# Attention and a Fourier-gated layer on one core: head pairs in seven key tiles, a written order on TensorE, folded transforms, a staged first batch

## The chip, the cores and the metric

The kernel runs on one NeuronCore of a Trainium2 chip. The core has TensorE (PE in the profile; its weight loads are PEld), VectorE (DVE), ScalarE (ACT), GpSimd (POOL) and SyncE (SP, which only issues DMAs here). Each engine takes its own instructions in the order in which they stand in its queue, and waits on semaphores for the others. The metric is the device time of one execution in microseconds.

## The reference

Batch 8, 12 heads, 448 positions, head size 64, so a model width D of 768. All inputs and the output are float32; the kernel's products run in bfloat16.

```python
scores = scale * np.matmul(q, k.transpose(0, 1, 3, 2))
m = np.max(scores, axis=-1, keepdims=True)
e = np.exp(scores - m)
attn = e / (np.sum(e, axis=-1, keepdims=True) + np.exp(-m) + 1e-09)
return np.matmul(attn, v)
...
x = attn_out.transpose(0, 2, 1, 3).reshape(B, S, H * D)
...
proj = x @ w_proj                      # three parts of 768 columns: x1, x2, x3
X2 = np.fft.rfft(x2, n=S, axis=1)
H = np.fft.rfft(filter_fft, n=S, axis=0)[None, :, :]
x2_conv = np.fft.irfft(X2 * H, n=S, axis=1)
y = x1 * x2_conv * x3
return (y @ w_out)
```

Both kernels leave out the maximum, since exp(s) / (sum of exp(s) + 1) is the same number. The Fourier transforms are matrix products with tables of cosines and sines.

## The kernel before

Setup builds the tables in four pages (cosine and sine, frequencies 0 to 127 and 128 to 224), loads filter, w_out and w_proj in float32 over SP and casts them on DVE, and computes the filter's spectrum `hh`.

Per batch, `attn_load` brings q, k and v through POOL's queue, cast to bfloat16 by the DMA: 12 loads of 112 positions × 12 heads × 64, in runs of 256 bytes. Positions are cut into four tiles of 112. For each of the six head pairs, `attn_pair_scores` transposes q and k of both heads on PE into one 128-row tile, copies k into two tiles that are zero in the other head's half (`kTA`, `kTB`, cleared by POOL), and makes 8 score products of 448 columns, each with one exp on ACT (`ET`). `attn_pair_O` makes 32 products of 65 columns (64 of v and a column of ones for the row sum) into `oph`, and DVE divides (`rec`, `xb`). `attn_finish` transposes the result into `xT`.

`hyena_chunks` is the dense part of a batch, in six pieces: `proj_x1`, `proj_x3`, `proj_x2` (x2 with positions on the rows), `spectrum` (32 products `xr`, `xi`, and for each pair of pages six DVE products with `hh`), `idft_gate` (24 products `cps` of 448 columns) and `write_out` (48 products `ops`). `run_attention_with_chunks` places one piece of batch b behind the scores of each pair of batch b + 1. The order of instructions on every engine is then made by the tile framework's scheduler from that program. PSUM is one pool with two banks for each of four uses: transposes (`tr`), scores (`sc`), attention output (`op`), dense (`hy`).

Of the kernel before, what the change touches and what calls it, by code (L numbers as in the profile page):

```python
# [10 lines left out]
AF = mybir.ActivationFunctionType  # L12
# [10 lines left out]
NDT = D // 128  # L23
SCALE = 1.0 / float(np.sqrt(DH))
DCH = 384

PAGE_K0 = [0, 0, 128, 128]
PAGE_W = [128, 128, 97, 97]
PAGE_COS = [True, False, True, False]
FT_COL0 = [0, 128, 256, 353]  # L30
FT_NCOL = 450
# [3 lines left out]
def kernel(  # L35
# [12 lines left out]
    TWO_PI = float(2.0 * np.pi)  # L48
    SIN_SHRINK = 1.0 - 2e-6
    sin_scale = (TWO_PI / S) * SIN_SHRINK  # L50
    sin_bias = -float(np.pi) * SIN_SHRINK
# [7 lines left out]
    ident_f32 = const.tile([128, 128], F32, name="ident_f32")  # L59
    make_identity(nc, ident_f32)  # L60
    sin_bias_t = const.tile([128, 1], F32, name="sin_bias_t")
    exp_bias = const.tile([128, 1], F32, name="exp_bias")
    nc.vector.memset(sin_bias_t, sin_bias)
    nrow = const.tile([128, S], F32, name="nrow")
    kvec = []

    ft = wts.tile([SP, NST, FT_NCOL], BF16, name="ft")
    bt = wts.tile([128, 4, S], BF16, name="bt")
    wproj_bf = wts.tile([128, NDT, 3 * D], BF16, name="wproj_bf")
    wout_bf = wts.tile([128, NDT, D], BF16, name="wout_bf")  # L70
    filt_bf = wts.tile([SP, NST, D], BF16, name="filt_bf")
    hh = wts.tile([128, 4, D], BF16, name="hh")

    ld = ctx.enter_context(tc.tile_pool(name="ld", bufs=4))
    vextp = ctx.enter_context(tc.tile_pool(name="vextp", bufs=2))
    qktp = ctx.enter_context(tc.tile_pool(name="qktp", bufs=2))
    etp = ctx.enter_context(tc.tile_pool(name="etp", bufs=12))
    xbp = ctx.enter_context(tc.tile_pool(name="xbp", bufs=2))
    xtp = ctx.enter_context(tc.tile_pool(name="xtp", bufs=2))
    hyp = ctx.enter_context(tc.tile_pool(name="hyp", bufs=1))  # L80
    ytp = ctx.enter_context(tc.tile_pool(name="ytp", bufs=1))
    otp = ctx.enter_context(tc.tile_pool(name="otp", bufs=2))
    small = ctx.enter_context(tc.tile_pool(name="small", bufs=3))
    stmp_w = ctx.enter_context(tc.tile_pool(name="stmp_w", bufs=2))

    def setup_constants_and_weights():
        with tc.tile_pool(name="stmp", bufs=1) as stmp:
# [426 lines left out]
```

## Time and profile before

| | us |
|---|---|
| median of 3 runs (621.81, 623.59, 626.63) | 623.59 |
| span of the profiled execution | 615.7 |
| PE matmul busy | 541.6 (88%), 4336 instructions |
| DVE busy | 347.8 (56%) |
| ACT busy | 278.1 (45%) |
| POOL busy | 145.6 (24%) |
| HBM read, written | 43.84 MB, 11.01 MB |

The profile is of one execution; its span runs from its first to its last instruction, and its own time with what lies around the span is not among the runs' times, whose median is 7.9 us above the span. A row of a group reads: line, engine, operation, output<-inputs with their shapes, xcount, then busy us and mean ns of one, then idle time of the engine before it and what ended it. "L291" is line 291 of the kernel. The mean of a matmul is its latency: matmuls overlap, and the chain's pieces (a length for several matmuls in a row) show their pace. Rows of stages give busy us and count for each engine, the granted PE clock, the mean DMA share and GB/s.

### The profile page before, as it was taken

Reading aid. Unit: us, or ns where it says so; the run is one execution under the profiler, and the core shown is the slowest. Engines: PE = TensorE matmul, PEld = TensorE weight load, DVE = VectorE, ACT = ScalarE, POOL = GpSimd, SP = SyncE. Lnnn points to the kernel's source line nnn. Section 1 sums busy time; section 2 is a strip of 40 time slices with the busy share of each in tenths; the row PEclk is TensorE's granted clock in tenths of the full one; section 3 lists DMA queues with packets and bytes.
Section 4 is the critical chain, followed back from the end, with each engine's and each line's share of the span. In section 5 each row is a group of like instructions: output and inputs, shape, how many; then the busy total and the mean of one; then the engine's idle time right before and its main releaser. Section 6 shows DMA issues by size and latency. Waiting matters only on the chain.

```text
span 615.7 us, 10809 instructions
## 1 busy us (share of the span) xinstructions
PE 541.6 (88%) x4336; PEld 367.8 (60%) x4336; DVE 347.8 (56%) x929; ACT 278.1 (45%) x527; POOL 145.6 (24%) x237
## 2 busy tenths in 40 slices
PE   0127889999999899989999899989999999989977
PEld 0014665766667575757667566757576666757544
DVE  4743545475464935394656746393647546493572
ACT  0106775436436255536355453545453643735112
POOL 3533263033211522033301531052212300100000
PEclk9997898999999999999999999999999999999999
DMA  9999097029900985069900991088901920002002
GB/s 235 235 209 204 1 92 46 1 16 98 113 1 2 79 124 25 2 40 97 91 1 1 91 124 12 1 55 117 56 1 13 101 69 1 1 1 90 2 1 89
DMA packets 137810, 39.04 MB, mean 63 GB/s; under 512 B 131424, under 2 KB 131424, under 8 KB 137760
## 3 DMA queue, kind: packets, MB, share of 16 engines
q0 software_dynamic: 130560, 16.52, 46.6%
q1 hardware_dynamic: 7200, 21.83, 12.0%
q8 instruction: 34, 0.56, 0.4%
q14 instruction: 16, 0.13, 0.1%
HBM read 43.84 MB, written 11.01 MB: 89 GB/s over the span
## 4 chain that ended last, share of the span: by engine, by line
PE 78%; DVE 11%; DMA 6%; ACT 4%; issue 1%; DVEq 0%
PE scps L271 14%; PE oph L291 12%; PE ops L444 10%; PE pps L360 10%; PE pps L345 9%; PE pps L331 9%; PE cps L424 4%; ACT ET L277 4%; DMA w<-in_moe_w_proj_dram 4%; PE xr L378 3%; PE xi L387 3%; DMA f<-in_moe_filter_fft_dram 3%; DVE t L399 2%; PE ktps L255 1%; DVE t L408 1%; PE xtps L315 1%
## 5 line engine op out<-in xcount | busy, mean ns | idle before, releaser
L277 ACT ACTIVATE ET<-scps,exp_bias 112x448 bf16<-112x448 f32 x384 | 217.3, 635 | 214.9 <-PE scps L271 209.3
L291 PEld LDWEIGHTS <-ET 112*112 112x112 bf16 x1536 | 98.0, 133 | 18.1 <-issue 5.3
L291 PE MATMUL oph<-vext,ET 112*112 112x65 bf16 x1536 | 101.8, 217 | 0.7
L299 DVE TENSOR_SCALAR rec<-oph 112x4 f32<-112x4 f32 x96 | 15.2, 158 | 137.4 <-PE oph L291 136.3
L262 POOL MEMSET kTA<- 64x448 bf16 x48 | 22.5, 469 | 236.8 <-PE scps L271 223.0
L444 PE MATMUL ops<-wout_bf,yT 128*112 128x384 bf16 x384 | 74.3, 326 | 0.0
L271 PE MATMUL scps<-qT,kTB 128*112 128x448 bf16 x192 | 69.0, 359 | 4.9 <-DVE kTB L265 2.7
L360 PE MATMUL pps<-wproj_bf,xT 128*112 128x384 bf16 x384 | 72.9, 326 | 0.0
L271 PE MATMUL scps<-qT,kTA 128*112 128x448 bf16 x192 | 69.4, 361 | 3.4 <-DVE kTA L264 1.6
L331 PE MATMUL pps<-xT,wproj_bf 128*128 128x448 bf16 x288 | 71.8, 354 | 0.1
L345 PE MATMUL pps<-xT,wproj_bf 128*128 128x448 bf16 x288 | 64.6, 352 | 0.0
L444 PEld LDWEIGHTS <-yT 128*112 128x112 bf16 x384 | 48.5, 129 | 15.9 <-issue 1.8
L360 PEld LDWEIGHTS <-xT 128*112 128x112 bf16 x384 | 48.6, 129 | 15.7 <-issue 1.5
L424 PE MATMUL cps<-bt,yhat 128*128 128x448 bf16 x192 | 44.9, 351 | 9.2 <-DVE t L408 9.0
L367 ACT CAST x2n<-pps 112x384 bf16<-112x384 f32 x64 | 29.9, 480 | 37.6 <-PE pps L360 37.6
L451 ACT COPY osb<-ops 112x384 f32<-112x384 f32 x64 | 29.8, 480 | 37.1 <-PE ops L444 26.4
L338 DVE CAST x1T<-pps 128x448 bf16<-128x448 f32 x48 | 29.9, 624 | 28.9 <-PE pps L331 28.6
L352 DVE CAST x3T<-pps 128x448 bf16<-128x448 f32 x48 | 30.0, 624 | 23.4 <-PE pps L345 22.3
L345 PEld LDWEIGHTS <-wproj_bf 128*128 128x128 bf16 x288 | 27.9, 98 | 24.8 <-issue 2.8
L301 DVE TENSOR_TENSOR xb<-oph,rec 112x256 bf16<-112x256 f32 x96 | 40.1, 418 | 1.9
L331 PEld LDWEIGHTS <-wproj_bf 128*128 128x128 bf16 x288 | 27.5, 98 | 20.9 <-issue 3.0
L227 POOL DMA_DIRECT2D vext<-in_v_dram x32 | 31.4, 986 | 32.4 <-PE xtps L315 28.2
(68 smaller groups left out, 632.2 us busy)
## 6 DMA issues: line engine op xcount, KB each, us to landing
out_dram<-osb SPq DMA_DIRECT2D x32, 336.0 KB, 2.7
w<-in_moe_w_proj_dram SPq DMA_DIRECT2D x12, 576.0 KB, 7.0
qf<-in_q_dram POOLq DMA_DIRECT2D x32, 168.0 KB, 5.4
kf<-in_k_dram POOLq DMA_DIRECT2D x32, 168.0 KB, 5.2
vext<-in_v_dram POOLq DMA_DIRECT2D x32, 168.0 KB, 6.1
wo<-in_moe_w_out_dram SPq DMA_DIRECT2D x6, 384.0 KB, 5.7
f<-in_moe_filter_fft_dram SPq DMA_DIRECT2D x4, 336.0 KB, 4.6
```

The source lines that it names most:

```text
L227: nc.gpsimd.dma_start(vext[:, st, :, 0:DH], v[b, :, st * SP : (st + 1) * SP, :].rearrange("h p d -> p h d"),)
L271: nc.tensor.matmul(scps, kT[:, i * SP : (i + 1) * SP], qT[:, :],)
L277: nc.scalar.activation(e, scps, AF.Exp, scale=SCALE, bias=exp_bias[:SP, 0:1])
L291: nc.tensor.matmul(oph[:, j, :], et[u][i][:, j * SP : (j + 1) * SP], vext[:, i, h, :], start=(i == 0), stop=(i == NST - 1),)
L301: nc.vector.tensor_tensor(xb[:, :, h, :], oph[:, :, 0:DH], rec[:].unsqueeze(2).to_broadcast([SP, NST, DH]), op=ALU.mult,)
L331: nc.tensor.matmul(pps, wproj_bf[:, kt, dt * 128 : (dt + 1) * 128], xT[:, kt, :], start=(kt == 0), stop=(kt == NDT - 1),)
L338: nc.vector.tensor_copy(hb["x1T"][:, dt, :], pps)
L345: nc.tensor.matmul(pps, wproj_bf[:, kt, 2 * D + dt * 128 : 2 * D + (dt + 1) * 128], xT[:, kt, :], start=(kt == 0), stop=(kt == NDT - 1),)
L352: nc.vector.tensor_copy(hb["x3T"][:, dt, :], pps)
L360: nc.tensor.matmul(pps[:SP, :DCH], xT[:, kt, st * SP : (st + 1) * SP], wproj_bf[:, kt, D + ch * DCH : D + (ch + 1) * DCH], start=(kt == 0) ...
L424: nc.tensor.matmul(cps, yhat[:W, pg, dt * 128 : (dt + 1) * 128], bt[:W, pg, :], start=(pg == 0), stop=(pg == 3),)
L444: nc.tensor.matmul(ops_[:SP, :DCH], yT[:, dt, st * SP : (st + 1) * SP], wout_bf[:, dt, ch * DCH : (ch + 1) * DCH], start=(dt == 0), stop=( ...
```

## The change

The kernel is written anew around the same mathematics.

- **Attention.** The 896 keys of a head pair are cut into seven tiles of 128: three of each head, and one that holds the last 64 keys of both. `kz` is a ring of three tiles with fixed zero halves. A pair makes 7 score products; two heads' products of a tile go into two neighbouring banks and share one exp of 896 elements. `attn_out` works on 128 queries at a time (the last tile overlaps the one before) with 128-column weights: 7 products for each of 4 query tiles, in two halves that use the one bank of `op`. Exps take no bias tile. POOL's clearing of `kTA` and `kTB` is gone.
- **Transforms.** `back` folds xT about its ends and middle on DVE (`u`, `w`, `xf`), so that even and odd frequencies, cosine and sine, are four separate blocks of 113 or 112. proj2 works on the folded x. The spectrum takes 8 products, each copied by ACT; the inverse takes 24 products of 224 columns, and ACT and DVE unfold them (`cw`, `cv`).
- **Order.** PE's and POOL's orders are as written; the scheduler orders the rest. `attention(b)` gives 48 units, `dense(b)` 36, each with a cost from a table; after each attention unit dense units of the batch before are put in while `owed` (1.9 times the attention cost) lasts. A last few are left for the next batch.
- **PSUM.** Scores: 2 × 2 banks; `op`: 1; everything else: 3 (`hy`).
- **Loads.** Batch 0's q, k and v come in float32 over SP in runs of 256 to 1024 bytes and are cast by DVE (k), ACT (q) and POOL (v). w_proj, filter and w_out come through POOL's queue, cast by the DMA. Later batches' 13 loads (4 of q, 8 of k, 1 of v) are issued at unit 8 of the batch before.

DVE, the head of the program, where the filter is used for the first time. Before, from the first transposed q to the first division (`w` is a float32 piece of w_proj):

```order
L251 COPY qT<-qtps 128x448 [waits PE_49]
L264 COPY kTA<-ktps 64x448 [waits PE_49]
L265 COPY kTB<-ktps 64x448
L204 CAST wproj_bf<-w_865 128x1152 [waits DMAHW4_49]
L204 CAST wproj_bf<-w_868 128x1152 [waits DMAHW5_49]
L264 COPY kTA<-ktps 64x448 [waits DVE_49,PE_49,Pool_49]
L251 COPY qT<-qtps 128x448 [waits PE_49]
L265 COPY kTB<-ktps 64x448 [waits DVE_49,Pool_49]
L299 TENSOR_SCALAR rec<-oph 112x4 [waits PE_49]
```

Now, from pair 2's transposes to the first division of pair 1 (`uw` is the filter's fold, `filt` the loaded filter, `xps` the transposed output of pair 0):

```order
L330 COPY kz_119<-tps 64x4x128 [waits PE_49]
L331 COPY kz_119<-tps 64x512
L334 COPY qT<-tps 128x4x112
L391 COPY xT<-xps 128x448 [waits PE_49]
L288 TENSOR_TENSOR uw<-filt 113x1536 [waits DMASW6_49,DMASW5_49,DMASW7_49,DMASW4_49,DMASW3_49]
L373 TENSOR_SCALAR rec<-op 128x4 [waits PE_49]
L289 TENSOR_TENSOR uw<-filt 113x1536
L374 RECIPROCAL rec<-rec 128x4 [waits DVE_49]
L375 TENSOR_TENSOR xb<-op,rec 128x2x128 [waits DVE_49]
```

Casts of w_proj pieces stood between the pairs; in their place the fold of the filter, with a wait for five loads of POOL's queue, stands ahead of pair 1's division.

PE, the middle of a batch: before, scores of a pair among the products of x1 of the batch before (`pps`):

```order
L331 MATMUL pps_2015<-xT,wproj_bf 128x448
L271 LDWEIGHTS kTA
L271 MATMUL scps<-qT,kTA 112x448
L331 LDWEIGHTS wproj_bf
L331 MATMUL pps_2015<-xT,wproj_bf 128x448
L271 LDWEIGHTS kTB
L271 MATMUL scps<-qT,kTB 112x448
```

Now, the last two scores of a pair, a unit of proj2 (`xf` is the folded x) and the first products of attn_out:

```order
L346 LDWEIGHTS kz_118
L346 MATMUL sc<-qT,kz_118 128x448
...
L440 LDWEIGHTS xf
L440 MATMUL pps_1004<-wproj_bf,xf 113x384
...
L360 LDWEIGHTS er
L360 MATMUL op<-vr_116,er 128x130
L365 LDWEIGHTS e
L365 MATMUL op<-vn_114,e 128x65
```

Single scores that alternated with single dense products now stand as blocks: four scores, six dense products, then fourteen of attn_out.

The core of the diff:

```diff
-    psum = ctx.enter_context(tc.tile_pool(name="psum", bufs=2, space=bass.MemoryType.PSUM))
+    psc = ctx.enter_context(tc.tile_pool(name="psc", bufs=2, space=bass.MemoryType.PSUM))
+    pop = ctx.enter_context(tc.tile_pool(name="pop", bufs=1, space=bass.MemoryType.PSUM))
+    phy = ctx.enter_context(tc.tile_pool(name="phy", bufs=3, space=bass.MemoryType.PSUM))
...
     def attn_load(b):
...
+            )
+        for u in range(2):
+            c = slice(64 * u, 64 * u + 64)
+            for t in range(3):
+                nc.gpsimd.dma_start(A["kn"][:, :, 1 + t, c], kr[:, :, 4 * u + t, :])
+            nc.gpsimd.dma_start(A["kn"][c, :, 0, c], kr[c, :, 3, :])
+        nc.gpsimd.dma_start(
+            A["vn"][:].rearrange("p g t d -> p (g t) d")[:, :, 0:DH],
+            v[b].rearrange("h s d -> (h s) d").rearrange("(n p) d -> p n d", p=128),
+        )
...
+    def first_casts(A, hp):
+        nc.vector.tensor_copy(
+            A["kn"][:, hp, 1:4, :].rearrange("p j (u d) -> p u j d", u=2), A["sk", hp]
+        )
+        nc.scalar.copy(
+            A["qf"][:, :, 2 * hp : 2 * hp + 2, :].rearrange("p j u d -> p u j d"), A["sq", hp]
+        )
+        for u in range(2):
+            nc.gpsimd.tensor_copy(
+                A["vn"][:, hp, 4 * u : 4 * u + 3, 0:DH], A["sv", hp][:, u]
+            )
...
+    def filter_spectrum(F):
+        uw = hyp.tile([FQ, 2, 2, D], BF16, name="uw", tag="g")
+        nc.vector.tensor_tensor(uw[:, 0, :, :], F[:, 0:3:2, :], F[:, 1:4:2, :], op=ALU.add)
+        nc.vector.tensor_tensor(uw[:, 1, :, :], F[:, 0:3:2, :], F[:, 1:4:2, :], op=ALU.subtract)
+        for pg in range(4):
...
+    def scores(A, hp, t):
+        P = A[hp]
+        sc = psc.tile([128, 2, 512], F32, name="sc")
+        if t:
+            for u in range(2):
+                nc.tensor.matmul(sc[:, u, 0:S], P["z"][:, (4 - t, 4 + t)[u], :], P["qT"])
+            e = etp.tile([128, 2, S], BF16, name="e")
+            nc.scalar.activation(e, sc[:, :, 0:S], AF.Exp, scale=SCALE)
+        else:
+            nc.tensor.matmul(sc[:, 0, 0:S], P["z"][:, 4, :], P["qT"])
+            e = erp.tile([128, S], BF16, name="er")
+            nc.scalar.activation(e, sc[:, 0, 0:S], AF.Exp, scale=SCALE)
+        P["e"].append(e)
+    def attn_out(A, hp, hf):
+        e = A[hp]["e"]
+        op = pop.tile([128, 2, 2, DH + 1], F32, name="op")
+        for i in range(2):
+            qs = slice(Q0[2 * hf + i], Q0[2 * hf + i] + 128)
+            nc.tensor.matmul(
+                op[:, i, :, :], e[0][:, qs], A["vr"][:, hp, :, :], start=True, stop=False
+            )
+            for u in range(2):
+                for t in range(3):
+                    nc.tensor.matmul(
+                        op[:, i, u, :],
+                        e[1 + t][:, u, qs],
+                        A["vn"][:, hp, 4 * u + t, :],
+                        start=False,
+                        stop=(u == 1 and t == 2),
+                    )
+        rec = small.tile([128, 2, 2], F32, name="rec")
+        nc.vector.tensor_scalar_add(rec, op[:, :, :, DH], 1.0)
+        nc.vector.reciprocal(rec, rec)
+        nc.vector.tensor_tensor(
...
+    def back(A, hp):
+        xT = A["xT"]
+        tps = phy.tile([128, 512], F32, name="xps", tag="hy")
+        tb = tps.bitcast(BF16)
+        for t in range(NST):
+            nc.tensor.transpose(
+                tb[:, Q0[t] : Q0[t] + 128], A["xb"][:, t, 2 * hp : 2 * hp + 2, :], ident_bf
+            )
+        nc.vector.tensor_copy(xT[:, hp, 0:S], tb[:, 0:S])
+        nc.gpsimd.tensor_copy(xT[:, hp, S : S + 2], xT[:, hp, 0:2])
+        if hp % 3 == 2:
+            ds = slice(hp - 2, hp + 1)
+            u = fold.tile([128, 3, HALF + 2], BF16, name="u")
+            w = fold.tile([128, 3, HALF + 2], BF16, name="w")
+            lo, hi = xT[:, ds, 0 : HALF + 2], xT[:, ds, HALF : S + 2]
+            nc.vector.tensor_tensor(u, lo, hi, op=ALU.add)
+            nc.vector.tensor_tensor(w, lo, hi, op=ALU.subtract)
+            for pg, (t, op) in enumerate(
+                ((u, ALU.add), (u, ALU.subtract), (w, ALU.subtract), (w, ALU.add))
+            ):
+                nc.vector.tensor_tensor(
+                    A["xf"][:, pg, ds, 0:FQ],
+                    t[:, :, 0:FQ],
+                    t[:, :, HALF : HALF - FQ : -1],
+                    op=op,
+                )
+    def attention(b):
+        A = state[b]
+        units = []
+        for hp in range(NHP):
+            for t in range(4):
+                units.append((0.38 if t else 0.19, lambda hp=hp, t=t: scores(A, hp, t)))
+                if t == 0:
+                    nb, nh = (b, hp + 1) if hp + 1 < NHP else (b + 1, 0)
+                    if nb < n_batches:
+                        units.append((0.42, lambda nb=nb, nh=nh: transposes(state[nb], nh)))
+                if t == 1:
+                    pb, ph = (b, hp - 1) if hp else (b - 1, NHP - 1)
+                    if pb >= 0:
+                        units.append((0.23, lambda pb=pb, ph=ph: back(state[pb], ph)))
+            for hf in range(2):
+                units.append((0.48, lambda hp=hp, hf=hf: attn_out(A, hp, hf)))
+        return units
...
+        def spectrum(par, ch):
...
+            cs = slice(ch * DCH, (ch + 1) * DCH)
+            xs = small.tile([FQ, 2, DCH], BF16, name="xs")
+            for rs in range(2):
+                pg = 2 * par + rs
+                xps = phy.tile([128, 512], F32, name="xsp", tag="hy")
+                nc.tensor.matmul(xps[:K, :DCH], ft[:, pg, :K], x2[:, pg, cs])
+                nc.scalar.copy(xs[:K, rs, :], xps[:K, :DCH])
+            t1 = small.tile([FQ, 2, DCH], BF16, name="t1")
+            t2 = small.tile([FQ, 2, DCH], BF16, name="t2")
+            nc.vector.tensor_tensor(t1[:K], xs[:K], hrs[:K, par, :, cs], op=ALU.mult)
+            nc.vector.tensor_tensor(t2[:K], xs[:K], hrs[:K, par, ::-1, cs], op=ALU.mult)
+            nc.vector.tensor_tensor(
+                yh[:K, par, 0, cs], t1[:K, 0, :], t1[:K, 1, :], op=ALU.subtract
+            )
+            nc.vector.tensor_tensor(yh[:K, par, 1, cs], t2[:K, 0, :], t2[:K, 1, :], op=ALU.add)
...
+        def inverse(dt):
...
+            for par in range(2):
+                K = BLK_K[2 * par]
+                for rs in range(2):
+                    nc.tensor.matmul(
+                        cps[:, par * HALF : (par + 1) * HALF],
+                        yh[:K, par, rs, dt * 128 : (dt + 1) * 128],
+                        bt[:K, 2 * par + rs, :],
+                        start=(rs == 0),
+                        stop=(rs == 1),
+                    )
+            nc.scalar.copy(cw[:, dt % 2, :, :], cps[:, 0:S].rearrange("p (a n) -> p a n", a=2))
+            if dt % 2 == 1:
+                cv = small.tile([128, 2, S], BF16, name="cv")
+                nc.vector.tensor_tensor(cv[:, :, 0:HALF], cw[:, :, 0, :], cw[:, :, 1, :], op=ALU.add)
+                nc.vector.tensor_tensor(
+                    cv[:, :, HALF:S], cw[:, :, 0, :], cw[:, :, 1, :], op=ALU.subtract
+                )
+                ds = slice(dt - 1, dt + 1)
+                nc.vector.tensor_tensor(yT[:, ds, :], g[:, ds, :], cv, op=ALU.mult)
...
+        U += gu(0)
+        for pg in range(4):
+            for ch in range(2):
+                U.append((0.97, lambda pg=pg, ch=ch: proj2(pg, ch)))
+        U += gu(1)
+        for par in range(2):
+            for ch in range(2):
+                U.append((0.33, lambda par=par, ch=ch: spectrum(par, ch)))
+            U += gu(2 + par)
+        for dt in range(2):
+            U.append((0.38, lambda dt=dt: inverse(dt)))
+        U += gu(4)
+        for dt in range(2, 4):
+            U.append((0.38, lambda dt=dt: inverse(dt)))
+        U += gu(5)
+        for dt in range(4, 6):
+            U.append((0.38, lambda dt=dt: inverse(dt)))
         for st in range(NST):
+            for ch in range(2):
+                U.append((0.97, lambda st=st, ch=ch: write_out(st, ch)))
...
         for hp in range(NHP):
+            first_casts(state[0], hp)
+            if hp == 2:
+                wproj_load(1)
+            if hp == 4:
+                wproj_load(0)
+                wproj_load(2)
+        F = filter_load()
+        state[1] = attn_load(1)
+        wout_load()
+        transposes(state[0], 0)
+        queue, owed = [], 0.0
+        for b in range(n_batches):
+            for i, (cost, emit) in enumerate(attention(b)):
+                emit()
+                if b and i == 5:
+                    if b == 1:
+                        filter_spectrum(F)
+                    queue += dense(state[b - 1])
+                if i == 8 and b and b + 1 < n_batches:
+                    state[b + 1] = attn_load(b + 1)
+                if i == 40 and b + 1 < n_batches:
+                    rest(state[b + 1])
+                if not queue:
+                    owed = 0.0
+                    continue
+                owed += cost * RATIO
+                while queue and owed >= queue[0][0] / 2:
+                    c, f = queue.pop(0)
+                    f()
+                    owed -= c
+        last = state[n_batches - 1]
+        back(last, NHP - 1)
+        for c, f in queue + dense(last):
+            f()
```

More of the change, by code (lines that the diff above doesn't have):

```diff
@@ L209, in attn_load @@
[L209 to L225 removed]
+    hrs = wts.tile([FQ, 2, 2, D], BF16, name="hrs")
@@ new lines @@
+    RATIO = 1.9
+    with (
+        tc.tile_pool(name="tabs", bufs=1) as tp,
+        tc.tile_pool(name="stage", bufs=3) as sp,
+        tc.manual_schedule(engines={mybir.EngineType.PE, mybir.EngineType.Pool}),
+    ):
+        state = {0: first_load(sp, tp)}
+        tables(tp)
+        first_rests(state[0])
+        F = None
+        for hp in range(NHP):
+            first_casts(state[0], hp)
[32 more added lines that the diff above has]
+            f()
```

677 lines of the change are left out of this document (287 added, 390 removed).

## The prediction, made before the changed kernel ran

> **What bounds the kernel now.** I read the stages first: busy time of each engine (PE, PEld, DVE, ACT, POOL, with instruction counts), the granted clock, the DMA share and GB/s.
>
> ```profile
> 0.00:60.00 60.00, 15.93 (x85) 10.02 (x86) 31.29 (x70) 12.86 (x22) 23.54 (x40) 0.96 1.49 222
> 221.40:289.20 67.80, 65.32 (x537) 44.44 (x536) 39.47 (x109) 33.42 (x64) 17.36 (x28) 1.00 0.60 52
> 560.60:615.70 55.10, 46.81 (x284) 29.91 (x282) 26.20 (x59) 9.61 (x21) 0.00 (x0) 0.99 0.14 44
> ```
>
> ```profile
> PE 78%; DVE 11%; DMA 6%; ACT 4%; issue 1%; DVEq 0%
> ```
>
> The head is bound by loads. In the middle stage PE is busy 65.3 of 67.8 us and ACT only 33.4. The last row is the share of each engine in the chain that ended last: 78% on PE. So a batch is worth what PE must stream plus what it waits. The chain in order of time (start, length, what) gives the pace of each kind of matmul:
>
> ```profile
> 98.83 2.84 PE pps L331 x15
> 221.35 3.92 PE ops L444 x24
> 234.01 3.03 PE pps L331 x16
> 237.04 1.63 PE oph L291 x32
> 238.67 0.20 PE qtps L245 x4
> 289.21 3.92 PE ops L444 x24
> 567.66 6.25 PE pps L331 x32
> 609.23 2.12 PE ops L444 x12
> ```
>
> 448 columns take 3.03/16 = 0.189 us, 384 take 0.163, so about 0.42 ns a column; a 112-column transpose 0.05; a 65-column oph 0.051. The period is 289.21 − 221.35 = 67.86 us. PE's stream in it: scores 48 × 0.189 = 9.1; oph 192 × 0.051 = 9.8; x1 and x3 72 × 0.189 = 13.6; x2 and write_out 96 × 0.163 = 15.6; spectrum 32 × 0.163 = 5.2; inverse 24 × 0.189 = 4.5; transposes 72 × 0.05 = 3.6. Sum 61.4, so 6.4 us a batch are lost. Dense work starts at 98.83 and the last matmul ends at 611.35; 4.35 us of copy and store follow.
>
> **The change, part by part: PE's stream.** Scores 42 × 0.189 = 7.9 (−1.2). Spectrum 8 × 0.163 = 1.3 (−3.9). Inverse 24 × 0.095 = 2.3, as 224 columns at 0.42 ns (−2.2). Transposes: 24 of 112 columns and 48 of 128, 3.8 (+0.2). The three projections and write_out keep their 29.2. attn_out becomes 24 matmuls of 130 columns (0.057 each, 1.4) and 144 of 65, whose price is open, because the weights are now 128 columns wide:
>
> ```profile
> L291 PEld LDWEIGHTS <-ET 112*112 112x112 bf16 x1536 | 98.0, 133 | 18.1 <-issue 5.3
> L331 PEld LDWEIGHTS <-wproj_bf 128*128 128x128 bf16 x288 | 27.5, 98 | 20.9 <-issue 3.0
> ```
>
> 112 columns load in 133 ns, 128 columns in 98: the wider load is the shorter one. If the load sets oph's 0.051, taking 35 ns less of it leaves the 65 columns themselves, 0.03. Bounds 0.03 to 0.051; I take 0.035, near the lower, since 65 columns at 0.42 ns are 0.027. So 144 × 0.035 = 5.0 and attn_out 6.4 (5.7 to 8.7; −3.4). The Trainium skill, "TensorE: Matmul & The Clock Gate", section on weight-path perf modes, says that a fast weight load is on when the weights are 128 columns and not FP32; the two rows agree with it. Without it the sum below would be 8 × 144 × 0.016 = 18 us longer. The new stream is 50.9 us: 10.5 less.
>
> **The change: what PE waits for.** PE now runs in a written order, so a late exp or a late drain of a bank stops everything. ACT:
>
> ```profile
> L277 ACT ACTIVATE ET<-scps,exp_bias 112x448 bf16<-112x448 f32 x384 | 217.3, 635 | 214.9 <-PE scps L271 209.3
> L367 ACT CAST x2n<-pps 112x384 bf16<-112x384 f32 x64 | 29.9, 480 | 37.6 <-PE pps L360 37.6
> L164 ACT ACTIVATE exp_bias<-tpages 97x1 f32<-97x1 f32 x1 | 0.2, 204 | 0.0
> 69.68 3.31 ACT ET L277 x6
> 75.00 3.31 ACT ET L277 x6
> ```
>
> An exp over two banks (896 elements) isn't in the trace. Above: two exps of 448 back to back, 2 × 3.31/6 = 1.10 us. Below: 1 element takes 204 ns and 384 take 480, 0.72 ns an element, so 0.204 + 895 × 0.72 = 0.85. I take 0.95, midway. ACT per batch: 18 × 0.95 + 6 × 0.55 + 24 copies × 0.48 + 12 of 448 × 0.53 = 38 us, under PE's stream. The DVE rows for the drains:
>
> ```profile
> L299 DVE TENSOR_SCALAR rec<-oph 112x4 f32<-112x4 f32 x96 | 15.2, 158 | 137.4 <-PE oph L291 136.3
> L300 DVE RECIPROCAL rec<-rec 112x4 f32<-112x4 f32 x96 | 16.7, 173 | 2.1
> L301 DVE TENSOR_TENSOR xb<-oph,rec 112x256 bf16<-112x256 f32 x96 | 40.1, 418 | 1.9
> L432 DVE TENSOR_TENSOR g<-x1T,x3T 128x448 bf16<-128x448 bf16 x48 | 18.0, 389 | 1.1
> L435 DVE TENSOR_TENSOR yT<-g,cps 128x448 bf16<-128x448 bf16 x48 | 29.1, 620 | 6.8 <-PE cps L424 5.3
> ```
>
> Four waits. (1) After scores t=3 two exps are left, 1.9 us; one dense unit (about 1.1) and the scores (0.4) cover 1.5: 0.4 × 6 pairs = 2.4. (2) op has one bank; a drain is 158 + 173 + 418 ns, about 0.9 with crossings; the second half of pair 0 has no dense unit ahead (0.9), pair 2 two short ones: 1.2. (3) Spectrum fills banks in 0.33 and ACT empties them in 2 × 0.48: four units, with the interleaved attention, 1.5. (4) write_out behind the last inverse: ACT 0.53, two cv and the yT product (0.39, 0.39, 0.6), less 1.2 of scores, transposes and first matmuls: 0.8. With 0.5 for the rest, 6.4, as much as now. All are laid one behind the other; hidden wholly they cost 0, and with every cover missing about 14. Period 50.9 + 6.4 = 57.3 us. DVE's work stays near its 39 us: folds and x1 products come, 16 f32 spectrum products go.
>
> **The change: the head.** The loads (a queue's packets, MB and share; stages, the second with POOL's busy time alone, then clock, DMA share and GB/s; POOL in order of time):
>
> ```profile
> q0 software_dynamic: 130560, 16.52, 46.6%
> 24.00:28.00 4.00, 0.19 (x1) 0.00 (x0) 2.46 (x7) 0.00 (x0) 0.62 (x1) 1.00 1.40 295
> 228.00:232.00 4.00, 1.09 (x3) 1.00 2.40 121
> 226.14 2.79 POOL L227 DMA_DIRECT2D vext<-in_v_dram  x3 [5.61 <-PE xtps L315]
> 231.72 0.16 POOL L231 MEMSET vext<- 112x12 bf16 x1 [2.79 <-DMA vext<-in_v_dram]
> 234.09 0.15 POOL L231 MEMSET vext<- 112x12 bf16 x1 [0.79 <-DMA vext<-in_v_dram]
> ```
>
> 46.6% over 8 batches reads as 36 us of DMA a batch, but shares go above 1 (2.40): packets overlap. The three v loads issued from 226.14 land by 231.72 and 234.09, two in 2.37 us, 1.2 each: a batch of twelve is 14 to 18 us. A batch's load is issued at unit 8 of 48 and wanted at unit 41, 33/48 × 57 = 39 us later: hidden, even at 36. POOL's queue then holds rest's copies, which wait for the v load; behind them stand back's two-element copies for pairs 4 and 5, wanted by a fold some 6 us later, so nothing late there. SP keeps only the stores. 1.2 us for 344 KB read is 290 GB/s, as the 295 of the head.
>
> In the new DVE queue, uw (the filter's fold) stands ahead of pair 1's first rec in batch 0, and waits for the filter, which POOL issues behind all of w_proj. Behind it wait op's drain, so PE, so pairs 1 to 5. Bytes ahead, by shapes in float32: 4.13 MB of q, k, v, 7.08 of w_proj, 1.39 of filter, 12.6 MB at 0.29 MB/us = 43.5 us, with start and landing 48 (61 at the 222 GB/s of the first row). Casting loads of long rows aren't in the trace; the 256-byte ones at 290 GB/s are the nearest. Then about 3.5 for uw and pair 1, four pairs of 5.5 (now 75.00 − 69.68 = 5.3): 73.5. Three us of attention(1) and the filter's spectrum (8 copies × 0.48 = 3.9) follow: dense work starts at 80.5, against 98.8 now.
>
> The idle PE comes back cold (busy columns as above, then clock):
>
> ```profile
> 52.00:56.00 4.00, 0.64 (x9) 0.42 (x6) 2.80 (x5) 2.43 (x3) 0.85 (x2) 0.87 1.87 227
> 56.00:60.00 4.00, 3.47 (x17) 2.39 (x16) 0.34 (x2) 2.53 (x5) 0.21 (x2) 0.50 2.07 268
> ```
>
> After 52 to 56, nearly idle, the clock is 0.50. Two pairs at half clock add 2 × 3 us at most; if it stayed cold until dense work starts, 10 us. The Trainium skill, same page, part 1, says that an idle window of about 3.4 us returns the clock to half; these rows agree.
>
> **Sum.** Dense work of batch 0 starts at 80.5; that of batch 6 six periods later, 424.3; attention(7) goes on for 52 behind that point (a period less 3.9 of units ahead of it and 1.4 that the last batch lacks), then 3.2 of leftover units: 479.5. The last dense part: 13.6 + 15.6 + 1.3 + 2.3 = 32.8, plus the 5.5 that today's loses (611.35 − 567.66 = 43.7 against a stream of 68 × 0.189 + 96 × 0.163 + 5.2 + 4.5 = 38.2). 517.8, and 4.35 of tail: a span of 522 us against 615.7. The runs' median 623.59 is 7.9 above the profiled span; I keep that: **530 us**.
>
> **Rivals.** (a) *The waits double.* Engines in fixed order add up each other's queues; 6.4 becomes 14: 530 + 7 × 7.6 = 583. For: ACT and DVE are both near 70% of the shorter period. Against: today's loss is 6.4 with the same kinds of waits. (b) *Head or weights fall short*: loads at 222 GB/s, +13, PE cold, +10; or weights of 128 columns no faster, +18: 540 to 553. (c) *Slower than before: the hy banks.* All dense products, transposes and back share three banks, 54 uses a batch. A use is filled (up to 1.1), waits on ACT or DVE behind an exp (0.95) or a run of spectrum products, and is copied (0.5 to 0.6): 2.6 us typically, while three banks in 57.3 us allow 3.2. If the mean hold were 4.0, the period would be 54 × 4.0/3 = 72 us: 530 + 7 × 14.7 = 633. It decides from a hold of 3.2 and crosses today's time at 3.9. Against: most holds end in one copy.
>
> **How the numbers follow.** Forecast 0.60 (500 to 556: periods of 53 to 61); (a) 0.17; (b) 0.14; today's time within 1% (hold 3.9) 0.03; (c) 0.06. One per cent is about what a measurement of this kernel can tell. So faster 0.91, same 0.03, slower 0.06. The range, 492 to 583, takes in the forecast, (b) and half of (a); its low end is every wait but 2 us hidden (a period of 52.9) and 7 us off the head, all loads at 295 GB/s and no cold PE.
>
> **What would show it.** Period near 57 between equal write_out matmuls; 65-column matmuls every 35 ns; first dense matmul near 80 with DVE waiting on the filter's load until 48; PE's waits named exp and rec, some 0.4 us each. The forecast is wrong if the period passes 62, if the hy banks are what PE waits for, or if a batch's loads land after unit 41.

## The result

The changed kernel takes 531.89 us (median of 4 runs, 529.51 to 533.56), the kernel before 622.92 on the same chip (4 runs, 621.81 to 626.63): a ratio of 0.854, 95% interval 0.850 to 0.859. The forecast was 530. The profiled execution took 532.04 us, 1.74 above its span of 530.3. Of all the runs below one was in a slow state (569.82 us, products on GpSimd); it is left out of the times and ratios.

### The profile page after: what moved, and what is told of

It is laid out like the page before. It is cut to its first block, busy times and chain, and to the rows that moved or that the text cites. A ratio compares the mean times of both kernels' runs of the same rounds, so it can differ in the third digit from the quotient of the medians.

```text
span 530.3 us, 9720 instructions
## 1 busy us (share of the span) xinstructions
PE 439.5 (83%) x3872; PEld 299.5 (56%) x3872; DVE 303.4 (57%) x881; ACT 292.7 (55%) x499; POOL 117.6 (22%) x184
## 4 chain that ended last, share of the span: by engine, by line
PE 52%; DVE 21%; ACT 13%; DMA 6%; issue 5%; SPq 1%; POOL 1%; ACTq 0%; DVEq 0%; POOLq 0%
PE ops L523 11%; PE pps L440 11%; PE pps L475 10%; ACT e L348 8%; PE op L365 6%; PE sc L346 5%; ACT cw L506 3%; DVE t L463 3%; DVE t L464 3%; DMA filt<-in_moe_filter_fft_dram 2%; PE op L360 2%; DVE xb L375 2%; PE xps L388 2%; DMA sv<-in_v_dram 2%; DVE g L486 2%
## 5 line engine op out<-in xcount | busy, mean ns | idle before, releaser
L348 ACT ACTIVATE e<-sc 128x896 bf16<-128x896 f32 x144 | 129.6, 920 | 20.5 <-PE sc L346 19.0
L346 PE MATMUL sc<-qT,kz 128*128 128x448 bf16 x288 | 78.6, 365 | 4.5 <-ACT e L348 4.5
L365 PE MATMUL op<-vn,e 128*128 128x65 bf16 x1152 | 66.6, 197 | 17.3 <-ACT e L348 17.3
L475 PEld LDWEIGHTS <-wproj_bf 128*128 128x128 bf16 x576 | 53.8, 97 | 46.4 <-issue 0.8
L440 PE MATMUL pps<-wproj_bf,xf 128*113 128x384 bf16 x384 | 72.0, 327 | 0.0
L365 PEld LDWEIGHTS <-e 128*128 128x128 bf16 x1152 | 54.5, 99 | 26.6 <-ACT e L348 22.2
L360 PE MATMUL op<-vr,er 128*128 128x130 bf16 x192 | 43.1, 225 | 27.6 <-DVE xb L375 27.6
L440 PEld LDWEIGHTS <-xf 128*113 128x113 bf16 x384 | 48.4, 132 | 12.6
L486 DVE TENSOR_TENSOR g<-x,pps 128x448 bf16<-128x448 bf16 x48 | 29.7, 618 | 39.5 <-PE pps L475 39.5
L447 ACT CAST x<-pps 113x384 bf16<-113x384 f32 x64 | 30.7, 480 | 34.7 <-PE pps L440 34.3
L375 DVE TENSOR_TENSOR xb<-op,rec 128x256 bf16<-128x256 f32 x96 | 40.7, 424 | 3.2
```

What stands on the lines that cost most here:

```text
L346: nc.tensor.matmul(sc[:, u, 0:S], P["z"][:, (4 - t, 4 + t)[u], :], P["qT"])
L348: nc.scalar.activation(e, sc[:, :, 0:S], AF.Exp, scale=SCALE)
L360: nc.tensor.matmul(op[:, i, :, :], e[0][:, qs], A["vr"][:, hp, :, :], start=True, stop=False)
L365: nc.tensor.matmul(op[:, i, u, :], e[1 + t][:, u, qs], A["vn"][:, hp, 4 * u + t, :], start=False, stop=(u == 1 and t == 2),)
L375: nc.vector.tensor_tensor(A["xb"][:, 2 * hf : 2 * hf + 2, 2 * hp : 2 * hp + 2, :], op[:, :, :, 0:DH], rec[:].unsqueeze(3).to_broadcast([12 ...
L440: nc.tensor.matmul(pps[:FQ, :DCH], xf[:, pg, kt, 0:FQ], wproj_bf[:, kt, D + ch * DCH : D + (ch + 1) * DCH], start=(kt == 0), stop=(kt == N ...
```

## The profile after

The stages as the prediction read them (us, then PE, PEld, DVE, ACT, POOL busy with instruction counts, clock, DMA share, GB/s): the head up to the first dense matmul, one period, and the last dense part.

```profile
0.00:79.50 79.50, 35.78 (x321) 23.90 (x322) 46.45 (x135) 33.32 (x46) 32.95 (x56) 0.85 1.02 148
121.50:180.37 58.87, 53.08 (x488) 36.37 (x485) 35.09 (x104) 34.95 (x60) 14.37 (x21) 1.00 0.65 60
489.43:530.30 40.87, 34.29 (x201) 22.75 (x199) 13.56 (x31) 17.67 (x37) 0.00 (x0) 0.99 0.15 48
```

The head is 19.3 us shorter (79.5 for 98.8), the period 9.0 us (58.87 for 67.86). PE is busy for 90% of a period, before for 96%: the stream got shorter, and more is waited for. The share of the engines in the chain that ended last (the chain of work followed back from the last instruction) says the same. Before, PE held 78% of it and ACT 4%:

```profile
PE 52%; DVE 21%; ACT 13%; DMA 6%; issue 5%; SPq 1%; POOL 1%; ACTq 0%; DVEq 0%; POOLq 0%
```

PE's waits in that period (line, who is waited for: us, times, longest), as PE's matmuls and as its weight loads see them. `xb` is the division's result, which frees the bank of `op`; `e` an exp; `yT` the gated product that write_out reads; `qT` the copy that frees a `hy` bank after the transposes. "Issue" is idle time for which the profile names nobody:

```profile
PE op L360 <- DVE xb L375: 2.0, 2, 1.0
PE op L365 <- ACT e L348: 1.8, 4, 0.9
PE ops L523 <- DVE yT L514: 1.0, 1, 1.0
PE xsp L459 <- DVE qT L338: 0.7, 1, 0.7
...
```

```profile
PEld L360 <- DVE xb L375: 3.7, 6, 1.3
PEld L365 <- ACT e L348: 2.2, 4, 1.1
PEld L523 <- DVE yT L514: 1.4, 1, 1.4
PEld L459 <- DVE qT L338: 1.1, 1, 1.1
PEld L388 <- issue: 0.4, 1, 0.4
```

A weight load runs ahead of its matmul, so its wait begins earlier: these rows come to 8.8 us, while PE's matmuls leave 5.8 of the period idle (58.87 − 53.08). The largest wait is for op's single bank. The chain of waits gives the pace of the new pieces (start, length, what):

```profile
137.93 1.73 ACT e L348 x2
141.66 0.19 PE op L365 x6
...
518.76 7.37 PE ops L523 x44
```

An exp of 896 elements goes every 1.73/2 = 0.865 us; a 65-column matmul every 31.5 ns or so (0.19/6); the last matmul ends at 526.1. In the head, DVE in order of time [idle before, and what ended it], and the matmul that stood behind it:

```profile
42.69 0.96 DVE L288 TENSOR_TENSOR uw<-filt 113x1536 bf16<-113x1536 bf16 x1 [8.27 <-DMA filt<-in_moe_filter_fft_dram]
```

```profile
45.19 0.29 PE L360 MATMUL op<-vr,er 128*128 128x130 bf16 x1 [8.77 <-DVE xb L375]
```

This is the stall that the prediction foresaw: the filter's fold ahead of pair 1's division, PE idle for 8.8 us.

## The experiments

The theory after the first reading: a period is PE's stream and the waits of a written order; the largest of these waits is for VectorE, which in pairs 2 and 3 is busy for 12.8 of 14.3 us. Ratios are to the kernel before, which ran with each set (medians of 620.7 to 623.9 us); the changed kernel's is 0.854. "Dense" is where the first dense matmul starts.

| kernel | us | ratio (95%) | dense | period |
|---|---|---|---|---|
| changed kernel | 531.9 | 0.854 (0.850–0.859) | 79.5 | 58.9 |
| filter first | 522.4 | 0.838 (0.833–0.842) | 68.6 | 58.9 |
| query tiles of 112 | 552.1 | 0.885 (0.881–0.890) | 84.6 | 61.3 |
| spectrum matmuls × 4 | 543.0 | 0.869 (0.865–0.874) | 81.7 | 59.8 |
| two op banks, two hy | 533.7 | 0.857 (0.852–0.862) | 73.8 | 59.4 |
| spectrum spread | 533.4 | 0.859 (0.856–0.861) | 79.3 | 59.0 |
| products on GpSimd | 564.4 | 0.908 (0.902–0.913) | 79.2 | 62.1 |
| casting first load, filter first | 527.9 | 0.849 (0.846–0.853) | 75.3 | 58.9 |
| attn_out later | 509.6 | 0.818 (0.816–0.821) | 74.8 | 55.8 |
| PE and POOL free | 488.7 | 0.787 (0.784–0.789) | 72.2 | 53.8 |
| PE free | 483.7 | 0.776 (0.774–0.778) | 68.6 | 53.8 |
| PE and POOL free, filter first | 485.5 | 0.778 (0.776–0.781) | 64.9 | 53.8 |
| PE free, filter first | 482.0 | 0.777 (0.773–0.781) | 65.2 | 53.8 |

### The filter ahead of the weights

```diff
+            if hp == 2:
+                F = filter_load()
                 wproj_load(1)
...
-        F = filter_load()
```

(and the tables' sines get a tile of their own)

> The filter's five transfers are issued ahead of all weights (behind them only batch 0's). Theory (the fold uw stands on VectorE ahead of pair 1's reciprocal, and TensorE stood 8.8 us until the filter landed at 42.7): this stall goes, TensorE's clock stays up through pair 1, dense(0) starts at 69 to 71 in place of 79.5, and the kernel takes 521 to 524 (ratio to the kernel after 0.98). Rival (the first 80 us are bound by the loads that all have to come anyway): the stall moves to another transfer (batch 1's queries or the weights), dense(0) starts at 76 or later, 528 or more.

522.36 us; the span is 11.0 us shorter, and dense work starts 10.9 earlier. The period stays at 58.87. The fold in this kernel, from the view of the tile `filt` (shortest/median/longest in ns, then the first and last start in us):

```profile
L288 DVE TENSOR_TENSOR uw<-filt x1: 958/958/958, 23.5 to 23.5; 113x1536 bf16<-113x1536 bf16 x1
```

It runs at 23.5 in place of 42.7, VectorE waits 0.7 us for the filter in place of 8.3, and the clock of the head is 0.95 where it was 0.85. The theory holds: no wait of PE in this head names a load that was pushed back. They had little room, though. The chain that ended last now runs for 18 us through batch 1's queries, behind which GpSimd's two-column copies stand, and VectorE waits 0.7 us for such copies before a fold.

### Weights of 112 columns again

```diff
-Q0 = [0, 128, 256, 320]
+Q0 = [0, 112, 224, 336]
```

(with xb, op and rec of 112 partitions)

> Query tiles of attn_out are 112 columns without overlap, as in the kernel before, in place of 128 that overlap. Theory (the 65-column matmul goes at 31.5 ns since its weights are 128 wide, and would go at 51 ns as before): 144 x 19.5 ns = 2.8 us more per batch, and half as much again on the 130-column one; 553 to 558. Rival (their width counts for nothing, and the drop from 51 to 31.5 ns came from another order of the matmuls): within 2 us of the kernel after, 530 to 534, or below it since VectorE's evictions have fewer rows.

552.14 us, 20.2 more. The weight loads of this kernel over the whole run, then a piece of its chain:

```profile
L365 PEld LDWEIGHTS <-e 128*112 128x112 bf16 x1152 | 80.3, 137 | 23.9 <-ACT e L348 21.3 <-issue 0.2
```

```profile
181.50 0.29 PE op L365 x6
```

The load takes 137 ns for 99, and a 65-column matmul 0.29/6 = 48 ns for 31.5. 144 × 16.8 ns = 2.4 us, and the period grew by 2.45. The profiled span grew by 22.2: 17.2 in the six periods and the last batch's attention, at 2.45 each, and 5.1 ahead of the first dense matmul, more than this price explains. So the width of the weights sets this pace, and these matmuls lie on the path.

### More PE work in pairs 2 and 3

```diff
-                nc.tensor.matmul(xps[:K, :DCH], ft[:, pg, :K], x2[:, pg, cs])
+                for _ in range(4):
+                    nc.tensor.matmul(xps[:K, :DCH], ft[:, pg, :K], x2[:, pg, cs])
```

> Each spectrum matmul is issued four times (the output stays as it is): 24 more of 0.163 us per batch, 3.9 us on TensorE and nothing on any other engine. Theory A (the period is TensorE's stream plus waits that stay): 8 x 3.9 = 31 us more, 563. Theory B (TensorE waits in pairs 2 and 3 for VectorE's queue, in which the spectrum's products stand ahead of the reciprocal and the qT copy; added matmuls there only fill that wait): about 2.5 us per batch are taken out of the waits for xb and qT, some 11 to 16 us more in all, 543 to 548.

542.96 us, 11 more: theory B, at the low edge of what it gave. The period takes 0.95 of the added 3.9 us; the rest fell into waits that were there (in the weight loads' rows 1.8 us for xb in place of 3.7, and 0.2 for qT in place of 1.1). In the last dense part, which has no attention beside it, 3.0 of the 3.9 show. So PE has slack in pairs 2 and 3. That suggests that the folded spectrum, priced at −3.9 us a batch, is worth less than its price in the written order; a run that adds matmuls doesn't show what taking them away gave.

### Two banks for op

```diff
-    pop = ctx.enter_context(tc.tile_pool(name="pop", bufs=1, space=bass.MemoryType.PSUM))
-    phy = ctx.enter_context(tc.tile_pool(name="phy", bufs=3, space=bass.MemoryType.PSUM))
+    pop = ctx.enter_context(tc.tile_pool(name="pop", bufs=2, space=bass.MemoryType.PSUM))
+    phy = ctx.enter_context(tc.tile_pool(name="phy", bufs=2, space=bass.MemoryType.PSUM))
```

> Two op banks and two hy banks in place of one and three. Theory (the single op bank's drain costs 3.7 us a period, and hy banks have slack): up to 3 us per batch less, 508 to 520. Rival, rival c of the prediction in its weaker form (a hy bank is held 2.3 to 4 us from its first matmul to its eviction, some 40 units of them a batch, so two hy banks can carry no more than one unit each 1.2 to 2 us): the wait goes over to the hy banks, 560 or more.

533.67 us: neither the gain nor the loss that was expected. Its weight loads wait, in one period:

```profile
PEld L365 <- ACT e L348: 2.2, 4, 1.1
PEld L523 <- DVE yT L514: 1.0, 1, 1.0
PEld L459 <- DVE qT L338: 0.9, 1, 0.9
PEld L523 <- DVE qT L338: 0.7, 2, 0.4
PEld L388 <- issue: 0.7, 2, 0.4
PEld L388 <- DVE qT L338: 0.7, 2, 0.4
PEld L459 <- issue: 0.6, 2, 0.3
PEld L499 <- issue: 0.6, 1, 0.6
...
PEld L440 <- DVE qT L338: 0.3, 1, 0.3
```

The wait for xb (3.7 us) is gone. In its place stand waits for qT, 2.6 us for 1.1, and idle time for which the profile names nobody, 3.5 us over all its rows for 0.4. The head won 5.8 us, six periods lost 3.4 and the end of the program 3.9. So a second bank for op, paid for with one of hy, gains nothing. What it would gain with three hy banks kept isn't shown, as the run changed both.

### Spreading the spectrum

```diff
-        U += gu(1)
+        between = gu(1) + gu(2)
         for par in range(2):
             for ch in range(2):
                 U.append((0.33, lambda par=par, ch=ch: spectrum(par, ch)))
-            U += gu(2 + par)
+                U.append(between.pop(0))
+        U += gu(3)
```

> The four spectrum units stand with one gate unit behind each, in place of two side by side and two gates behind them; the work is the same. Theory (in pairs 2 and 3 VectorE runs 12 us without a gap, with 6.0 us of spectrum products in runs of 3 us ahead of the reciprocal and the qT copy, and TensorE waits 1.0 + 0.7 us and more for them): the runs are 1.5 us long, of the 4.8 us of waits for xb and qT in a period 1.5 to 3 go; 508 to 520. Rival (the wait is the op bank's own drain of 0.9 us, six times a period, whatever else VectorE has): 529 to 533.

533.44 us: no gain, where the rival gave 529 to 533. In PE's rows the wait for qT went, and those for xb and exp grew (2.0 and 1.8 in the changed kernel):

```profile
PE op L360 <- DVE xb L375: 2.5, 2, 1.6
PE op L365 <- ACT e L348: 2.4, 5, 0.9
...
```

Shorter runs of products moved the wait and did not take it away.

### Products to GpSimd

```diff
-            nc.vector.tensor_tensor(t2[:K], xs[:K], hrs[:K, par, ::-1, cs], op=ALU.mult)
+            nc.gpsimd.tensor_tensor(t2[:K], xs[:K], hrs[:K, par, ::-1, cs], op=ALU.mult)
...
-            nc.vector.tensor_tensor(yh[:K, par, 1, cs], t2[:K, 0, :], t2[:K, 1, :], op=ALU.add)
+            nc.gpsimd.tensor_tensor(yh[:K, par, 1, cs], t2[:K, 0, :], t2[:K, 1, :], op=ALU.add)
```

> The second product t2 and the second half of yh are computed on GpSimd in place of VectorE: 8 operations, 3.3 us at VectorE's pitch, leave its queue per batch. Theory (VectorE's queue in pairs 2 and 3 is what TensorE waits for there): 2 to 3 us of the period of 58.9 go, 508 to 516, unless GpSimd needs more than about 2.5 us per unit, in which case the first inverse waits for yh. Rival (the drain of the op bank by itself): 529 to 533. Second rival (both engines share a port, and GpSimd's operations slow VectorE's down): 535 or more, with VectorE's L463 above 0.55 us in the rows.

564.35 us, the second rival. Groups of this kernel, then of the changed kernel:

```profile
L464 POOL TENSOR_TENSOR t<-xs,hrs 113x768 bf16<-113x768 bf16 (+1 forms) x32 | 75.4, 2355 | 58.1 <-ACT xs L460 58.1
L465 DVE TENSOR_TENSOR yh<-t 113x384 bf16<-113x384 bf16 (+1 forms) x32 | 39.2, 1225 | 0.6
L463 DVE TENSOR_TENSOR t<-xs,hrs 113x768 bf16<-113x768 bf16 (+1 forms) x32 | 32.4, 1012 | 1.7 <-ACT xs L460 1.5
```

```profile
L465 DVE TENSOR_TENSOR yh<-t 113x384 bf16<-113x384 bf16 x16 | 5.6, 352 | 0.0
L463 DVE TENSOR_TENSOR t<-xs,hrs 113x768 bf16<-113x768 bf16 x16 | 8.9, 555 | 1.3 <-ACT xs L460 0.4
```

GpSimd needs 2.36 us for what VectorE does in 0.55, and with it VectorE's own operations take 1.01 for 0.55 and 1.23 for 0.35 on average. VectorE's busy time in a period is 37.9 us, more than the 35.1 of the changed kernel. So this run says nothing on the theory: it did not relieve VectorE.

### The written order taken away

```diff
-        tc.manual_schedule(engines={mybir.EngineType.PE, mybir.EngineType.Pool}),
```

> The order of TensorE and GpSimd isn't held to the program's; the scheduler orders them by its own costs, as it does VectorE and ScalarE. What the fixed interleave is worth. Theory (the written order covers exp and the evictions by dense units, which the scheduler's own costs don't know): waits of 8.8 us per period become 12 or more; 550 to 600. Rival (both orders are about the same, since the emission order is a priority anyway): 528 to 536.

488.73 us, 43 less than with the written order. Theory and rival were both wrong: the theory expected a loss. One period of PE is now 53.8 us. To see which engine's order it is, PE alone was freed:

```diff
-        tc.manual_schedule(engines={mybir.EngineType.PE, mybir.EngineType.Pool}),
+        tc.manual_schedule(engines={mybir.EngineType.Pool}),
```

> TensorE's order is left to the scheduler, GpSimd's stays as written. Theory (the 43 us that the free order gained are TensorE's waits): 486 to 493, with a period of about 53.8. Rival (a part of it comes from GpSimd's queue, in which loads and the two-column copies of xT stand): 495 or more, the difference then being in the first 80 us or in the waits for the fold.

483.65 us. PE's order is the cause. GpSimd's written order is worth some 5 us: the first scores start at 21.3 and not 29.7, dense work at 68.6 and not 72.2. (The scheduler orders VectorE in all these kernels, and its order follows PE's a little: of its 103 operations in a period some ten stand elsewhere. No run holds VectorE's order fixed while PE's is freed.) A period of this kernel, and the waits of its matmuls:

```profile
121.39:175.18 53.79, 52.91 (x483) 35.69 (x482) 34.60 (x104) 34.51 (x61) 14.11 (x21) 1.00 0.71 66
```

```profile
PE op L360 <- DVE xb L375: 0.6, 2, 0.5
PE ops L523 <- DVE yT L514: 0.2, 1, 0.2
```

PE, DVE and ACT are busy for 52.9, 34.6 and 34.5 us, much as in the changed kernel's period (53.1, 35.1, 35.0); what went is idle time. The weight loads still wait, 4.9 us for 8.8, of which 2.2 are for xb: the change is that PE's matmuls seldom run dry meanwhile. The stretch of pairs 2 and 3 shows how, in the changed kernel first, then with PE free:

```profile
158.67:173.00 14.33, 11.31 (x113) 6.79 (x111) 12.77 (x38) 7.87 (x15) 0.45 (x1) 1.00 0.01 2
```

```profile
140.19:154.50 14.31, 13.66 (x128) 8.26 (x125) 13.36 (x41) 9.89 (x19) 0.19 (x1) 1.00 0.01 2
```

VectorE is even busier there (13.4 of 14.3 us), and PE is busy for 13.7 us and not 11.3. VectorE's queue got no shorter: from the division at 159.31 to the one at 171.08 it needs 11.8 us in the changed kernel, and 12.0 for the same stretch with PE free (140.84 to 152.82). In this stretch PE does wait for VectorE, as the theory said; the remedy was other work for PE to do meanwhile, and not a shorter queue. PE in order of time, in the changed kernel:

```profile
168.10 0.23 PE L365 MATMUL op<-vn,e 128*128 128x65 bf16 x2
169.27 0.30 PE L365 MATMUL op<-vn,e 128*128 128x65 bf16 x4 [0.95 <-ACT e L348]
...
169.65 1.30 PE L475 MATMUL pps<-xT,wproj_bf 128*128 128x448 bf16 x6
170.79 0.55 PE L499 MATMUL cps<-bt,yh 113*128 113x224 bf16 x4
172.36 0.23 PE L360 MATMUL op<-vr,er 128*128 128x130 bf16 x1 [1.02 <-DVE xb L375]
```

and at the same place with PE free:

```profile
147.32 0.41 PE L365 MATMUL op<-vn,e 128*128 128x65 bf16 x2
147.57 0.35 PE L350 MATMUL sc<-qT,kz 128*128 128x448 bf16 x1
147.80 0.32 PE L459 MATMUL xsp<-x,ft 113*112 113x384 bf16 x1
147.97 1.68 PE L475 MATMUL pps<-xT,wproj_bf 128*128 128x448 bf16 x8
149.52 0.30 PE L365 MATMUL op<-vn,e 128*128 128x65 bf16 x4
```

Where the written order stands still for 0.95 us on an exp, between the second and the third product, the free one puts a score of the next pair, a spectrum matmul and eight of a gate. It cuts units apart; the written order moves them whole.

### Distance in a written order

```diff
+                pb, ph = (b, hp - 1) if hp else (b - 1, NHP - 1)
...
+                if t < 2 and pb >= 0:
+                    units.append((0.48, lambda pb=pb, ph=ph, t=t: attn_out(state[pb], ph, t)))
+                if t == 2 and pb >= 0:
+                    units.append((0.23, lambda pb=pb, ph=ph: back(state[pb], ph)))
...
-            for hf in range(2):
-                units.append((0.48, lambda hp=hp, hf=hf: attn_out(A, hp, hf)))
```

(pb, ph: the pair before; the last pair's attn_out follows the loop, and the dense queue opens two units later)

> The written order stays, but the two attn_out units of a pair stand behind the first and the second scores unit of the next pair, and back behind the third, in place of close behind their own exp. The work is the same. Theory (a written order loses because attn_out stands right behind the exp that it reads and its second half right behind the eviction of the first; more distance covers both): of 8.8 us of waits in a period 4 to 6 go, the period comes to 53.5 to 55.5 from 58.9, 495 to 510. Rival (in an order of whole units that each wait in turn, what one covers the next one loses, as two op banks and the spread spectrum did, which moved the wait and gained nothing): 525 to 536.

509.6 us, inside the theory's range; the period is 55.83, 3.0 less and just outside of it. PE's wait for exp is gone:

```profile
PE ops L522 <- DVE yT L513: 1.1, 1, 1.1
PE pps L474 <- ACT xs L459: 0.8, 1, 0.8
PE op L360 <- DVE xb L375: 0.7, 2, 0.5
...
```

So a written order isn't bound to lose: distance alone takes 3.0 of the 5.1 us a period that the free order takes. Whether the other 2 come from cutting units apart or from a better place for whole ones wasn't tried.

### How batch 0 comes in

```diff
-        state = {0: first_load(sp, tp)}
+        state = {0: attn_load(0)}
...
-        first_rests(state[0])
+        rest(state[0])
...
-            first_casts(state[0], hp)
```

> As the kernel with the filter loaded first (522.4), but batch 0 comes by the casting transfers that the other batches use, in place of f32 over SyncE with casts on the engines. Theory (the first 20 us are bound by bytes that have to come either way; the permuted qT copy of 1.15 us in place of 0.39 and the casts go): 3 to 6 us less, 516 to 520. Rival (casting transfers of 128-byte packets are slower, 1.2 us per 344 KB at best, and all stand in one queue, so that the first scores come at 28 or later in place of 21): 527 to 535.

527.9 us, 1.1% above its base, the kernel with the filter first (1.4% by the ratios): staging batch 0 in float32 is worth some 5 to 7 us. The rival's reason was wrong, though. The first scores came at 16.5, earlier than the base's 21.8. What came late stood behind them: the filter (VectorE waited 2.4 us for it), the rests of v (PE 2.3) and the fold of pairs 0 to 2, which waited 3.3 us for a two-column copy on GpSimd, whose queue now held batch 0's loads too. Dense work started at 75.3 for 68.6.

### What helped, together

> The free order (488.7) and the filter loaded first (9.5 us less in the written order). Theory (in the free order TensorE still stands 15 us at the head for the qT copy behind the filter's fold on VectorE): 478 to 483. Rival (the free order has already taken what the loads of the head allow; the stall goes to batch 1's transfers): 486 to 490.

> TensorE's order left to the scheduler, GpSimd's as written, and the filter loaded first: the three that helped, together. Theory (the period stays at 53.8 and of the 16 us in which TensorE stands between 25 and 69 us in the kernel with TensorE's order alone free, half goes with the filter): 474 to 479. Rival (the head's transfers are the bound once TensorE follows them, as with both engines free, where the filter first gave 3 us and not 9.5): 481 to 486.

485.45 and 481.98 us, ratios of 0.778 and 0.777 against 0.776 for PE free alone. With both engines free the filter first gains 3.3 us, between what theory and rival gave; with PE alone free it gains nothing that the ratios show, though dense work starts 3.4 us earlier, and the time lies in the rival's range. In that last head PE has a new wait,

```profile
PE tps L320 <- DMA kn<-in_k_dram: 5.1, 1, 5.1
```

for batch 1's keys, whose transfers had been pushed back. The kernels at 0.776 to 0.778 are the fastest here, 9% below the changed kernel.

## Why the prediction was right, and where it was lucky

**The stream** was priced at 50.9 us. Its uncertain term, 144 matmuls of 65 columns at 35 ns, measured 31.5 (−0.5 us), and the run with 112 columns shows that the reason was right too: the width of the weights. With PE free, PE is busy for 52.9 us of a period, so 50.9 was short by 2 us at most. Of the −10.5 only attn_out's −3.4 was tested by a run. The rest, the folded transforms above all, goes by counts and by paces that the trace shows as priced: 189 ns for 448 columns, 163 for 384, 98 for 224.

**The waits** were sized 6.4 us. They measure 8.8 in the weight loads' rows, or 8.5 as the prediction reckoned them, period less stream (58.87 − 50.4). Of its four waits: exp ahead of attn_out 2.4, measured 2.2; write_out behind the last inverse 0.8, measured 1.4; spectrum banks 1.5, measured 1.1, though named qT and not ScalarE's copies; *the single op bank 1.2, measured 3.7*. This is the step that failed: the drain was counted as its three operations (0.9 us) and charged at two pairs of six, with VectorE free to take them. The trace shows a wait for it at all six pairs. Three are short (0.2 to 0.3 us); the two longest, 1.05 and 1.28, come where the division stands in VectorE's queue behind folds and spectrum products. The period came to 58.87 for 57.3.

A second thing was missed beside the size. The prediction priced the waits inside a written order, at "as much as now", and did not ask what that order costs against the scheduler's. The run with PE free answers it: of PE's 5.8 us of idle time in a period 0.9 are left, the period is 5.1 us shorter, and the head 10.9.

**The head.** Dense work was forecast at 80.5 and began at 79.5, from two misses that cancel: the filter landed at 42.7 and not 48 (−5.3), while the pairs behind it took 6.7 to 7.1 us and not 5.5 (+5.3 over four); what stands before and behind these pairs took 1.0 less. The first and the fourth of them, with the clock behind POOL's column:

```profile
46.06:53.20 7.14, 5.10 (x51) 3.53 (x49) 3.75 (x10) 3.08 (x4) 4.65 (x6) 0.74 1.65 106
66.70:73.40 6.70, 4.61 (x50) 3.04 (x48) 3.06 (x10) 3.08 (x4) 0.19 (x1) 0.84 0.00 0
```

With the filter first, a pair at clock 1.00 (36.53 to 42.34) takes 5.8 us and one at 0.84 (55.73 to 62.66) 6.9. So 5.5 was a little short, and the cold PE, a rival's price of +10, came in part. The stall of 8.8 us is not its only cause, as the clock falls in that head too, which has no such stall.

**The sum.** Head −1.0; six periods 6 × 1.57 = +9.4; attention(7) 56.7 for 55.2, +1.5; the last dense part 36.7 for 38.3, −1.6; tail −0.2: the span is 530.3 for 522.2, +8.1. The 7.9 us carried from span to time were wrong: every execution, of before too (620.95 with a span of 619.1), lies 1.7 to 1.9 above its span. By the same 1.8 the profiled execution before took some 617.5 us, 6 less than the median run, and this spread is what the 7.9 held. That is −6.2. The time was met within 2 us by errors of +8.1 and −6.2: that closeness is luck. With either error alone put right the forecast would have been 524 or 538, inside its own range of 500 to 556.

**The rivals.** (a) Waits doubled: the waits came to 8.8 and not 14. PE's idle time in the busy rows did double, from 2.5 to 5.8, but no term was reckoned by it. (b) The weights of 128 columns were as fast as priced and the filter came early; only the cold clock of this rival showed. (c) The hy banks: with two in place of three the period is 59.4, so 54 uses of mean hold h need 54 × h / 2 to be at most 59.4, and h is at most 2.2 us there. In the changed kernel's own trace the 53 uses that a period shows whole are held for 1.6 us on average, from first matmul to end of eviction. The 2.6 "typically" was too long, and so were the 2.3 to 4 us in the expectation for two op banks. The rival was further off than its 0.06. The loads of later batches stayed hidden.

## What to carry to other kernels

A wait that an engine's rows show in a written order names who was late, not what to change. Here another split of the banks and other places for the late work moved the wait on, while distance between a product and its reader took 3.0 us of a period away, and the scheduler's order 5.1. Before one engine's order is written out by hand, run the free order once: the change won 91 us with the hand order and 43 to 48 more without it. And add errors with their signs: a total that fits can hold two that cancel.

## What the runs showed of the hardware

- VectorE is slowed while GpSimd computes: with products on both, VectorE's 0.55 us product took 1.01 and its 0.35 us one 1.23 on average. What GpSimd's 2.36 us would be without VectorE beside it isn't shown. The Trainium skill, "SBUF — State Buffer", section "SBUF: two separate sides", says that a VectorE operation with two SBUF inputs and a GpSimd operation that reads SBUF take a shared port pair as an exclusive lock, and that the one that comes second is blocked until the other ends. The trace agrees: GpSimd's product ran from 163.27 to 165.27, and VectorE's, begun at 163.81, ended at 165.49, after 1.68 us for 0.35.
- Sixteen more weight columns make the 65-column matmul faster, as the prediction had reckoned: one went every 31.5 ns with 128-column weights and every 48 with 112, with loads of 99 and 137 ns.
